# Chunk 0 of a three-stage kernel: a written order, filler products and wider queries

## The chip, the cores and the metric

The kernel runs on one core of a Trainium2 chip. Its engines work side by side, each through its own list of instructions in order: TensorE (PE: products, and its weight loads PEld), VectorE (DVE), ScalarE (ACT), GpSimd (POOL) and SyncE (SP, which here issues most DMAs). The metric is the device time of one execution in microseconds; lower is better.

## The reference

```python
kv  = einsum('bhsd,bhse->bhde', k, v)       # 8 batches, 8 heads, 576 tokens, 64 wide
out = einsum('bhsd,bhde->bhse', q, kv)
out = out / sqrt(mean(out*out, -1) + 1e-6) * g_norm
x   = out as [4608 tokens, 512]
h   = max(x @ w1, x @ w2, x @ w3)           # 512 -> 768
x   = h @ w_out                             # 768 -> 512
# then 8 experts: noisy gate, top 2 of 8, per expert relu(x @ w1[e]) @ w2[e], weighted sum
```

## The kernel before

The 4608 tokens are done in nine chunks of 512. For each chunk `ao` multiplies the queries with the K-V matrix of their batch, `norm_sq` (ACT, L230), `norm_red` (DVE, L234), `norm_b1` (DVE L238, then Ln and Exp on ACT L239 and L240), `norm_b2` (DVE, L244 to L246) and `norm_c` (DVE, L250) normalise it, `xtrans` turns it (PE L272) and splits it into a high and a low part (`xtrans_hi` ACT L276, `xtrans_lo` DVE L281). Projections are three products: high by high, and the two crossed ones. `g1` (L353) makes 18 groups of 128 columns, of which each three are joined by a maximum; `g2` (L399) is the output projection and the gate's logits. Chunks 1 to 8 run through `for g in range(18)` with the next chunk's attention woven in: at `g == 12` `attend` calls both halves of `ao`. After them the experts run, in units of up to 512 tokens.

`kv_all` makes the K-V matrix of a batch: 40 calls of `kv_mm` (L187), 32 of them with 128 tokens and 8 with the last 64. K and V of a batch come in three loads: `KV0`, `STG[2]` and `kvr`. A float32 call of `PE.matmul` becomes two load-and-product pairs in the trace. `ao(c, j)` (L213) does half a chunk, two blocks of 128 tokens; the held (stationary) operand is a piece of queries, 64 deep and 64 tokens wide, and the streamed one is the 64x64 K-V matrix of a head. A batch has 576 tokens, so 64 is the largest width that never meets two batches.

Chunk 0 has a schedule of its own, since the weights must be rebuilt first. Each of the twelve weight stages `s` arrives as 64-bit words (`w{s}`, SP) and goes through `lo` (ACT L502), `op` (DVE L506, L507), `sq` (ACT L511), `add` (DVE L515), `top` (DVE L528), `hi` (ACT L532) and `rest` (DVE L536). Meanwhile PE has the passes of chunk 0 (`first...`: groups 0 and 1 by halves of 256 tokens; `gp`, `gq`: groups 2 to 17), of the first half of chunk 1 (`eq`, with maxima `ee`), the second batch's K-V matrix (`kvp3`), chunk 1's `ao0` and `ao1`, the gate's weights (`gate_...`) and the output passes (`out...`). Each is a `task` with an engine, an assumed cost and the tasks it comes after; `run_tasks` lays them out greedily by those costs, and what it emits is each engine's order. Ahead of it stand the first loads, conversion of stage 0, K-V of batch 0, both halves of `ao` of chunk 0 and their first norm steps, and `warm(7)`, which are products (L576) whose result nobody reads.

Of the kernel before, what the change touches and what calls it, by code (L numbers as in the profile page):

```python
# [72 lines left out]
def unit_order():  # L73
    seq = [("S", 0), ("S", 1)]
    small = [("1", 0), ("2", 0), ("T", 1), ("1", 1)]
    for i in range(N4):
        seq.append(("4", i))
        if i % 2 and small:
            seq.append(small.pop(0))
    return seq + [("H", 0), ("J", 2), ("2", 1)], [("1", i) for i in range(N1_MAIN, N1)]  # L80


def body(tc, A, dbg=None):
# [81 lines left out]
    def qv(c):  # L165
        return qbuf[c][:, 0:2048].rearrange("p (a t) -> p a t", a=4)
# [4 lines left out]
    pad = st("pad", [128, XW])  # L171
    POOL.memset(ones, 1.0)
# [217 lines left out]
    def g2(c, i, f0, f1):  # L390
        if f0 == 0:
            x2b[i] = abank(), abank()
        s = slice(i * 128, (i + 1) * 128)
        for f in range(f0, f1):
            h = hTf(f)
            w = wo(f // 2)[:, :, f % 2]
            for n, (a, b) in enumerate(((0, 0), (0, 1), (1, 0))):
                for z, (lo, hi) in enumerate(((0, 256), (256, 528))):
                    PE.matmul(x2b[i][z][:, 0:hi - lo], h[:, a, s], w[:, b, lo:hi],  # L399
                              start=f == 0 and n == 0, stop=f == 5 and n == 2)  # L400
        if f1 == 6:
            DVE.tensor_copy(lgs[:, i, :], x2b[i][1][:, 256:272])
            for z in range(2):
                b = x2b[i][z].bitcast(U16).rearrange("p (n t) -> p n t", t=2)
                for q in range(2):
                    (ACT.copy if q else DVE.tensor_copy)(  # L406
                        planes[:, i, q * 512 + z * 256:q * 512 + z * 256 + 256], b[:, 0:256, q])

# [128 lines left out]

    def gate_a(j, ring):
        t, d = wsrc(9 + j), wstage(9 + j)
        for ff in range(2):  # L540
            TR = ring()
            for k in range(4):
                PE.transpose(TR[:, k * 128:(k + 1) * 128], t[:, ff * 512 + k * 128:ff * 512 + (k + 1) * 128], ident)
            ACT.activation(d[:, ff * 512:ff * 512 + 512], TR, AF.Copy)

    gate_of = {}
# [33 lines left out]
    load_q(0)  # L580
# [37 lines left out]
    tasks, ring_users = [], []  # L618

    def task(name, eng, cost, after, fn, urgency=0, hb=None):  # L620
        tasks.append((name, eng, cost, after, fn, urgency, hb))

    def run_tasks(free, end):
        while tasks:
            best = None
            for x in tasks:
                name, eng, cost, after, fn, urgency, hb = x
                need = list(after)
                if hb:
                    taken = ring_users + [hb] * hb[1]  # L630
                    need += [u[0] for u in taken[:-4]]
                if any(n not in end for n in need):
                    continue
                at = max([free[eng]] + [end[n][0] + 0.1 * (end[n][1] != eng) for n in need])
                key = (at, urgency)
                if best is None or at < best[0][0] - 0.3 or (at < best[0][0] + 0.3 and urgency < best[0][1]):
                    best = (key, x)
            assert best, [x[0] for x in tasks]
            (at, _), x = best
            tasks.remove(x)  # L640
            name, eng, cost, after, fn, urgency, hb = x
            fn()
            end[name] = at + cost + (2.0 if eng == "SP" else 0.0), eng
            free[eng] = at + cost
# [10 lines left out]
    task("n0b1", "DVE", 0.2, [], lambda: norm_b1(0, 0, 4), 0)  # L655
    task("n0e", "ACT", 0.5, ["n0b1"], lambda: None, 0)
    task("n0b2", "DVE", 0.65, ["n0e"], lambda: norm_b2(0, 0, 4), 0)
    for i in range(4):
        task(f"n0c{i}", "DVE", 0.65, ["n0b2"], lambda i=i: norm_c(0, i), 0)
# [4 lines left out]
        task(f"t0{i}", "PE", 0.44, [f"n0c{i | 1}"] + ([f"t0{i - 1}"] if i else []), t0, 0,  # L664
# [8 lines left out]
    task("kvp3", "PE", 2.3, ["kv1", "first100"], kv1, 1, on_ring("kvo", 4))  # L673
# [4 lines left out]
    for s in range(1, 12):  # L678
# [7 lines left out]
        task(f"lo{s}", "ACT", 1.15, [f"w{s}"] + ["n0e"] * (s == 1), lambda s=s: conv_lo(s), u)  # L686
        task(f"op{s}", "DVE", 1.92, [f"w{s}"] + free_t + ["n0c3"] * (s == 1), lambda s=s: conv_hi(s), u)
# [34 lines left out]
    for g in range(18):  # L722
        if g > 1:
            task(f"gp{g}", "PE", 1.82, ["x0l3", f"hi{g // 2}"] + done + ([f"gq{g - 1}"] if g > 2 else []),
# [3 lines left out]
        hm_free = [f"split{f - 1}"] if g % 3 == 0 and 0 < f < 4 else ["x1t1"] if g == 12 else []  # L728
# [10 lines left out]
    for i in range(2):  # L739
        if i == 0:  # L740
            task("ao0", "PE", 1.0, ["q1", "kvo", "x0l3", "ev0"] + done, lambda: ao(1, 0, [abank(), abank()]), 0)
        task(f"n1s{i}", "ACT", 0.6, ["ao0", "t03"], lambda i=i: norm_sq(1, i, x1[i]), 0.6)
        task(f"n1r{i}", "DVE", 0.69, [f"n1s{i}"], lambda i=i: norm_red(1, i), 0.6)
    task("n1b1", "DVE", 0.2, ["n1r0", "n1r1"], lambda: norm_b1(1, 0, 2), 0.5)
    task("n1e", "ACT", 0.5, ["n1b1"], lambda: None, 0.5)
# [16 lines left out]
    for e in range(18):  # L762
# [3 lines left out]
             [f"eq{e}", "x1t0", "x0h3"] + ([f"ee{e - 1}"] if e % 3 else []),  # L766
             lambda e=e: g1_top(e, bank_of["e", e][:, 0:256], early(e // 3)), 0.5)
    for j in range(3):
        task(f"gate_a{j}", "PE", 0.9, [f"top{9 + j}"] + ([f"gate_b{j - 1}"] if j else []),
             lambda j=j: gate_a(j, hbank), 1.5, on_ring(f"gate_a{j}", 2))  # L770
        task(f"gate_w{j}", "ACT", 1.2, [f"gate_a{j}"], lambda: None, 0)
# [10 lines left out]
    def ao_late():
        ao(1, 1, [hbank(), hbank()])
        for i in range(2):
            norm(1, 2 + i, RB[:, i * 512:i * 512 + 512])

    task("ao1", "PE", 1.0, ["rest11", "ao0"], ao_late, 3.5, on_ring("ao1", 2))
# [200 lines left out]
    for c in range(NCH):  # L988
# [425 lines left out]
def layout(q, k, v, g_norm, moe_w1, moe_w2, moe_w3, moe_w_out,  # L1414
# [6 lines left out]
    a["qT"] = qf.transpose(2, 1, 0, 3).reshape(NCH, 128, 2048)  # L1421
# [28 lines left out]
```

## Time and profile before

| | us |
|---|---|
| median of three timed runs | 1505.43 (1503.96 to 1508.12) |
| the profiled execution | 1503.61 |
| its span, first to last instruction | 1501.8 |
| PE busy in it | 1476.2 (98%) |
| DVE, ACT, POOL busy | 749.5, 644.2, 223.3 |
| mean granted clock of PE | 0.998 |

A busy PE is not PE at its peak: a product's end is modelled, and weight loads (PEld) lie beside products. Times in the rows are us from the span's start.

### The profile page before, as it was taken

What the parts mean: (1) busy time and instruction counts of PE and PEld (TensorE: products, weight loads), DVE (VectorE), ACT (ScalarE), POOL (GpSimd) and SP (SyncE); (2) the same over time, 40 slices, a digit from 0 to 9 for tenths busy, and PEclk for the clock granted to TensorE, in tenths of its full rate; (3) what the DMA queues carried; (4) which work ended last, traced back from release to release, by engine and by line L of the source; (5) the groups of instructions that cost most, each with busy time, mean ns of one, the idle gap of its engine ahead of it and who ended that gap; (6) DMA issues with size and microseconds to landing.
All of it is one profiled execution on the core that took longest, in us unless ns stands there. A gap on an engine that the chain in (4) does not pass through costs nothing.

```text
span 1501.8 us, 22899 instructions
## 1 busy us (share of the span) xinstructions
PE 1476.2 (98%) x9190; PEld 1260.4 (84%) x9190; DVE 749.5 (50%) x1513; ACT 644.2 (43%) x1020; POOL 223.3 (15%) x332
## 2 busy tenths in 40 slices
PE   6999999999999999999999999999999999999997
PEld 6889989898989888888888878887888888888886
DVE  6985545454444444458344454553454374444443
ACT  4653524242424233334444454544454364444443
POOL 0000111102020202023211102202211111110112
PEclk9999999999999999999999999999999999999999
DMA  7412435142332303083776668767565587554555
GB/s 315 144 70 99 152 117 149 72 149 86 126 114 99 121 29 122 0 240 107 200 200 140 173 217 227 194 186 199 135 162 137 147 216 196 132 135 140 139 121 108
DMA packets 160724, 218.43 MB, mean 145 GB/s; under 512 B 124320, under 2 KB 124704, under 8 KB 145120
## 3 DMA queue, kind: packets, MB, share of 16 engines
q1 hardware_dynamic: 140624, 165.14, 35.0%
q0 software_dynamic: 19984, 51.73, 15.1%
q8 instruction: 74, 1.21, 0.3%
q14 instruction: 42, 0.34, 0.1%
HBM read 137.86 MB, written 51.72 MB: 126 GB/s over the span
## 4 chain that ended last, share of the span: by engine, by line
PE 54%; POOL 0%; issue 0%; ACT 0%; POOLq 0%
PE bank L1242 26%; PE bank L1180 26%; PE bank L1194 1%; PE bank L1283 1%; PE bank L1298 0%; PE bank L399 0%; POOL out L1216 0%; PE bank L1205 0%; ACT W L334 0%; PE bank L1289 0%; ACT xn L1247 0%; POOLq L1398 0%; ACT RA L406 0%; PE bank L1136 0%; POOL spacer L1215 0%
## 5 line engine op out<-in xcount | busy, mean ns | idle before, releaser
L353 PE MATMUL bank<-B,W 128*128 128x512 f32 (+1 forms) x2184 | 453.1, 367 | 2.2 <-ACT W L532 2.1
L353 PEld LDWEIGHTS bank<-B,W 128*128 128x128 f32 x2184 | 376.4, 188 | 70.4 <-ACT W L532 2.5
L1242 PE MATMUL bank<-W,B 128*128 128x512 f32 x1704 | 411.2, 390 | 0.0
L1242 PEld LDWEIGHTS bank<-W,B 128*128 128x128 f32 x1704 | 318.6, 188 | 64.5
L1180 PE MATMUL bank<-B,W 128*128 128x512 f32 (+4 forms) x1536 | 361.0, 374 | 0.0
L1180 PEld LDWEIGHTS bank<-B,W 128*128 128x128 f32 x1536 | 278.1, 188 | 53.7 <-issue 4.4
L335 DVE TENSOR_TENSOR W<-G,W 128x1024 fp32r<-128x1024 f32 x168 | 203.0, 1224 | 121.8 <-ACT W L334 121.3
L1184 ACT ACTIVATE B<-bank 128x512 fp32r<-128x512 f32 (+4 forms) x152 | 85.8, 565 | 334.3 <-PE bank L1180 334.3
L1185 DVE SCALAR_TENSOR_TENSOR B<-bank,B 128x512 fp32r<-128x512 f32 (+4 forms) x152 | 98.7, 649 | 249.0 <-ACT B L1184 248.4
L334 ACT ACTIVATE W<-G 128x1024 fp32r<-128x1024 f32 x168 | 175.4, 1055 | 43.5 <-PE bank L1242 24.9
L399 PE MATMUL bank<-W,B 128*128 128x256 f32 (+1 forms) x1296 | 161.0, 284 | 0.4 <-DVE B L361 0.2
L399 PEld LDWEIGHTS bank<-W,B 128*128 128x128 f32 x1296 | 159.5, 188 | 1.6 <-ACT RA L406 0.5
L472 POOL DMA_INDIRECT Xg<-RA,si x72 | 70.7, 981 | 582.0 <-issue 403.7
L371 DVE TENSOR_TENSOR hm<-hm,bank 128x512 f32<-128x512 f32 (+1 forms) x107 | 69.6, 651 | 115.2 <-PE bank L353 109.8
L1216 POOL DMA_INDIRECT out<-xn,idt x36 | 59.2, 1644 | 402.9 <-ACT xn L1247 397.6
L357 ACT ACTIVATE B<-hm 128x512 fp32r<-128x512 f32 (+1 forms) x53 | 32.2, 607 | 172.4 <-DVE hm L371 172.4
L1180 PE MATMUL bank<-xlo,W 128*128 128x512 f32 (+2 forms) x288 | 73.3, 376 | 0.0
L1180 PEld LDWEIGHTS bank<-xlo,W 128*128 128x128 f32 x288 | 52.5, 188 | 9.8
L369 ACT ACTIVATE hm<-bank 128x512 f32<-128x512 f32 (+1 forms) x54 | 30.4, 564 | 64.1 <-PE bank L353 52.2
L406 ACT COPY RA<-bank 128x256 uint16<-128x256 uint16 x72 | 25.6, 372 | 68.6 <-DVE RA L406 63.2
L1216 POOL DMA_INDIRECT out<-hm,idt x20 | 31.9, 1593 | 131.2 <-ACT hm L1247 127.4
L361 DVE TENSOR_TENSOR B<-hm,B 128x512 fp32r<-128x512 f32 (+1 forms) x53 | 35.1, 661 | 32.2 <-ACT B L357 32.2
(230 smaller groups left out, 1034.8 us busy)
## 6 DMA issues: line engine op xcount, KB each, us to landing
G<-mw SPq DMA_DIRECT2D x84, 1024.0 KB, 5.1
G<-w1s SPq DMA_DIRECT2D x12, 1024.0 KB, 4.9
kv<-kv SPq DMA_DIRECT2D x8, 1024.0 KB, 7.1
G<-kv SPq DMA_DIRECT2D x8, 1024.0 KB, 9.2
RB<-qT SPq DMA_DIRECT2D x8, 1024.0 KB, 4.9
G<-mw SPq DMA_DIRECT2D x16, 512.0 KB, 6.4
out<-pad POOLq DMA_DIRECT2D x5, 1280.0 KB, 6.5
out<-pad POOLq DMA_DIRECT2D x2, 1536.0 KB, 6.7
```

Source lines behind the costliest of these rows:

```text
L334: ACT.activation(w[:, 0:1024], src, AF.Copy)
L335: DVE.tensor_tensor(w[:, 1024:2048], src, w[:, 0:1024].bitcast(F), op=OP.subtract)
L353: PE.matmul(bank[:, 0:t1 - t0], w_in(g)[:, a, k, s], x[b][:, k, t0:t1], start=n == 0 and k == 0, stop=n == 2 and k == 3)
L361: DVE.tensor_tensor(h[:, 1], hm, h[:, 0].bitcast(F), op=OP.subtract)
L371: DVE.tensor_tensor(hm, hm, bank, op=OP.max)
L399: PE.matmul(x2b[i][z][:, 0:hi - lo], h[:, a, s], w[:, b, lo:hi], start=f == 0 and n == 0, stop=f == 5 and n == 2)
L472: i = POOL.indirect_dma_start(out=Xg, out_offset=bass.IndirectOffsetOnAxis(ap=idx, axis=0), in_=src, in_offset=None)
L1180: PE.matmul(bank[:, 0:n], w[:, a, k, s], x[b][:, k, 0:n], start=z == 0, stop=z == 11)
L1184: ACT.activation(h[:, 0, 0:n], bank[:, 0:n], AF.Relu)
L1185: DVE.scalar_tensor_tensor(h[:, 1, 0:n], bank[:, 0:n], 0.0, h[:, 0, 0:n].bitcast(F), op0=OP.max, op1=OP.subtract)
L1216: d = POOL.indirect_dma_start(out=A["out"], out_offset=bass.IndirectOffsetOnAxis(ap=idt[u % 3][:, i:i + 1], axis=0), in_=y, in_offset=None ...
L1242: PE.matmul(obank[i], h[:, a, s], w[:, b, ff % 2, :], start=ff == 0 and n == 0, stop=ff == 7 and n == 2)
```

## The change

Chunk 0's attention also becomes tasks, cut so that each has one engine, and so are pieces of `gate_a`, `gate_d`, `g2` and of the norms of chunk 1. `run_tasks` no longer plans: it emits a written list, `ORDER`, and asserts that each task stands behind those it needs. Some needs are added to the graph. `empty` makes products of a zeroed tile ahead of K and V, between their halves and ahead of the queries; `warm` makes nine. The K-V products of batch 0 run by token block first. The queries are laid out in two halves, chunk 0's come in two loads, and `ao` holds 128 tokens at a time where both halves of a block are of one batch. The middle passes of `first...` change places.

```diff
+ORDER = """
+n0a0 n0s0 n0s1 n0a1 warm n0r0 n0r1 n0b10 n0s3 n0r3 n0s2 w1 n0r2 n0e0 n0b20 n0b11 n0e1 kv1 n0c1 n0c0 t00 x0h0 t01
+n0b21 w2 x0h1 n0c2 n0c3 t02 first000 x0l0 lo1 t03 first001 op1 x0h3 x0l3 first100 x0h2 first010 x0l2 x0l1 first110
+add1 sq1 lo2 top1 first011 kvp3 kvo q1 first002 op2 first101 first012 add2 w3 hi1 first111 first112 first102 ev0 gp2
+ev1 ao0 sq2 rest1 n1s1 n1s0 gq2 top2 hi2 n1r1 gp3 ev2 n1r0 gq3 n1b1 gp4 w4 n1e rest2 n1b2 n1c1 n1c0 hi_h0 x1t1
+split0 ev3 w5 op3 x1t0 gq4 x1h0 x1l0 x1h1 x1l1 ev4 lo3 sq3 gp5 gq5 lo4 eq0 add3 ev5 top3 eq1 eq2 ee0 op5 ee1 eq3 op4
+hi3 sq4 rest3 ee2 gp6 add4 ee3 eq4 hi_h1 top4 lo5 gq6 ee4 eq5 w6 gp7 gq7 split1 ee5 w7 ev6 add5 hi4 eq6 lo6 eq7 gp8
...
     def qv(c):
-        return qbuf[c][:, 0:2048].rearrange("p (a t) -> p a t", a=4)
+        return qbuf[c][:, 0:2048].rearrange("p (x a t) -> p x a t", x=2, a=4)
...
+    DVE.memset(XN[0], 0.0)
...
+    def empty(sizes):
+        for n in sizes:
+            PE.matmul(HB[3][:, 0:n], XN[0][:, 0:128], XN[0][:, 0:n], start=True, stop=True)
+
     def kv_all(b, banks):
-        for p in range(4):
-            for s in range(4):
-                kv_mm(b, p, s, banks[p][:, 0:64])
+        for p, s in ([(p, s) for s in range(4) for p in range(4)] if b == 0 else
+                     [(p, s) for p in range(4) for s in range(4)]):
+            if b == 0 and (p, s) == (0, 2):
+                empty([256] * 3)
+            kv_mm(b, p, s, banks[p][:, 0:64])
...
-                for x in range(2):
-                    t = t0 + x * 64
-                    kb = KB[(c * CT + t) // S % 2]
+                k = [KB[(c * CT + t) // S % 2] for t in (t0, t0 + 64)]
+                w = 128 if k[0] is k[1] else 64
+                for x in range(0, 128, w):
                     for h in range(2):
-                        PE.matmul(banks[h][HALF[x], o], qv(c)[HALF[h], p, t:t + 64],
-                                  kb[HALF[h], p * 64:(p + 1) * 64], start=True, stop=True)
+                        PE.matmul(banks[h][x:x + w, o], qv(c)[HALF[h], j, p, i * 128 + x:i * 128 + x + w],
+                                  k[x // 64][HALF[h], p * 64:(p + 1) * 64], start=True, stop=True)
...
-    load_q(0)
+    for i in range(2):
+        SP.dma_start(RB[:, i * 1024:i * 1024 + 1024], A["qT"][0][:, i * 1024:i * 1024 + 1024])
...
+    empty([512] * 4 + [320])
     first = [abank() for p in range(4)]
     kv_all(0, first)
+    empty([256])
     load_kv_first(1)
...
-    for j in range(2):
-        ao(0, j, [abank(), abank()])
-        for i in range(2):
-            norm_a(0, 2 * j + i)
-    warm(7)
...
+    def run_tasks(done):
+        for name in ORDER.split():
+            after, fn, hb = tasks.pop(name)
...
+            fn()
+            done.add(name)
...
+    for j in range(2):
+        task(f"n0a{j}", "PE", 1.05, [f"q0{j}"], lambda j=j: ao(0, j, [abank(), abank()]), 0)
+    task("warm", "PE", 4.05, ["n0a1"], lambda: warm(9), 0)
...
-    a["qT"] = qf.transpose(2, 1, 0, 3).reshape(NCH, 128, 2048)
+    a["qT"] = qf.reshape(4, 128, NCH, 2, 256).transpose(2, 1, 3, 0, 4).reshape(NCH, 128, 2048)
```

## Rows read from the trace of the kernel before

**Rows 1.** Waits of PE from 130 us on: line, releaser, total, times, longest.

```profile
PE bank L399 <- ACT RA L406: 0.2, 1, 0.2
```

**Rows 2.** Windows: stretch, busy us of each engine (instructions), granted clock, DMA.

```profile
10.50:14.60 4.10, 3.75 (x72) 3.50 (x72) 1.42 (x3) 1.14 (x2) 0.00 (x0) 1.00 0.95 374
27.70:30.00 2.30, 2.30 (x81) 2.20 (x80) 2.15 (x3) 1.25 (x1) 0.00 (x0) 1.00 0.00 0
```

**Rows 3.** Timeline of PE, 8 to 45 us: start, length, instructions, idle before and releaser.

```profile
8.26 0.69 PE L187 MATMUL bank<-kv 128*64 128x64 f32 x8 [8.26 <-DMA kv<-kv]
10.72 0.70 PE L187 MATMUL bank<-G 128*64 128x64 f32 x8 [1.77 <-DMA G<-kv]
...
13.91 0.56 PE L187 MATMUL bank<-hm 64*64 64x64 f32 x16
14.68 2.19 PE L213 MATMUL bank<-kvt,RB 64*64 64x64 f32 x128 [0.21 <-DVE kvt L198]
16.80 3.45 PE L576 MATMUL bank<-cst 128*128 128x270 f32 x14
21.61 1.48 PE L272 MATMUL bank<-cst,xn 128*128 128x128 f32 x10 [1.35 <-DVE xn L250]
...
23.83 3.97 PE L353 MATMUL bank<-B,W 128*128 128x256 f32 x28
...
36.56 3.02 PE L353 MATMUL bank<-B,W 128*128 128x512 f32 x12
41.67 2.11 PE L353 MATMUL bank<-B,W 128*128 128x512 f32 x8 [2.09 <-ACT W L532]
```

**Rows 4.** Timeline of PE in chunk 1: both halves of `ao` for chunk 2.

```profile
154.00 2.10 PE L213 MATMUL bank<-kvt,RB 64*64 64x64 f32 x128
```

**Rows 5.** Weight loads of the span by form: operand, count, busy us, mean ns.

```profile
L353 PEld LDWEIGHTS bank<-B,W 128*128 128x128 f32 x2184 | 376.4, 188 | 70.4 <-ACT W L532 2.5 <-issue 1.2 <-DVE B L281 0.3
...
L213 PEld LDWEIGHTS bank<-kvt,RB 64*64 64x64 f32 x1024 | 15.8, 135 | 2.6 <-issue 2.1 <-DVE kvt L198 0.3
...
L1136 PEld LDWEIGHTS bank<-cst,s 128*1 128x1 f32 x2 | 0.2, 82 | 0.2
```

**Rows 6.** Timeline of weight loads near 101 us: the four of one `gate_d`.

```profile
101.35 0.54 PEld L561 LDWEIGHTS bank<-cst,G 128*128 128x128 f32 x4
```

**Rows 7.** Timeline of SP's queue at the head: issue, its length.

```profile
2.15 0.77 SPq L571 DMA_DIRECT2D hm<-kvr  x1
2.96 0.48 SPq L169 DMA_DIRECT2D RB<-qT  x1
```

**Rows 8.** The same two DMAs: size and us from issue to landing.

```profile
RB<-qT SPq DMA_DIRECT2D x1, 1024.0 KB, 10.9
hm<-kvr SPq DMA_DIRECT2D x1, 256.0 KB, 9.2
```

**Rows 9.** Timeline of ACT, 15 to 42 us.

```profile
15.98 1.57 ACT L230 ACTIVATE xn<-bank 128x512 f32<-128x512 f32 x3 [1.13 <-PE bank L213]
...
22.48 2.46 ACT L276 ACTIVATE B<-bank,gn 128x512 fp32r<-128x512 f32 x4 [1.63 <-PE bank L272]
...
40.56 1.06 ACT L532 ACTIVATE W<-RA 128x1024 fp32r<-128x1024 f32 x1
```

**Rows 10.** Timeline of DVE, 20 to 41 us.

```profile
20.30 0.19 DVE L246 SCALAR_TENSOR_TENSOR stat<-stat 128x32 f32<-128x32 f32 x1
20.59 1.89 DVE L250 TENSOR_TENSOR xn<-bank,stat 128x512 f32<-128x512 f32 x3
...
35.57 0.69 DVE L371 TENSOR_TENSOR hm<-hm,bank 128x512 f32<-128x512 f32 x1
37.31 0.69 DVE L234 TENSOR_REDUCE stat<-xn 128x8 f32<-128x512 f32 x1 [1.05 <-ACT xn L230]
...
39.31 1.22 DVE L528 SCALAR_TENSOR_TENSOR RA<-G 128x1024 f32<-128x1024 f32 x1
```

More of the change, by code (lines that the diff above doesn't have):

```diff
@@ L234, in norm_red, with norm_b1, norm_e @@
         DVE.tensor_reduce(ST[:, 0, i, :], x.rearrange("p (h e) -> p h e", h=8), axis=AX.X, op=OP.add)
-    def norm_b1(c, i0, i1):
+    def norm_b1(c, i0, i1, now=True):
         s = [ST[:, r, i0:i1, :] for r in range(2)]
         DVE.tensor_scalar(s[0], s[0], 1.0 / 64, 1e-6, op0=OP.mult, op1=OP.add)
+        if now:
+            norm_e(c, i0, i1)
+    def norm_e(c, i0, i1):
+        s = [ST[:, r, i0:i1, :] for r in range(2)]
         ACT.activation(s[1], s[0], AF.Ln)
@@ L400, in g2, with g2_out @@
                               start=f == 0 and n == 0, stop=f == 5 and n == 2)
-        if f1 == 6:
-            DVE.tensor_copy(lgs[:, i, :], x2b[i][1][:, 256:272])
[L403 to L407, printed above, removed]
+        if f1 == 6 and (c > 0 or i > 1):
+            for q in range(2):
+                g2_out(i, q)
+    def g2_out(i, q):
+        if q == 0:
+            DVE.tensor_copy(lgs[:, i, :], x2b[i][1][:, 256:272])
+        for z in range(2):
+            b = x2b[i][z].bitcast(U16).rearrange("p (n t) -> p n t", t=2)
+            (ACT.copy if q else DVE.tensor_copy)(
+                planes[:, i, q * 512 + z * 256:q * 512 + z * 256 + 256], b[:, 0:256, q])
     lgs = st("lgs", [128, 4, 16])
@@ L536, in conv_rest, with gate_w @@
         DVE.tensor_tensor(lo, t, hi.bitcast(F), op=OP.subtract)
+    gate_of = {}
     def gate_a(j, ring):
-        t, d = wsrc(9 + j), wstage(9 + j)
-        for ff in range(2):
-            TR = ring()
+        t = wsrc(9 + j)
+        gate_of["a", j] = [ring() for ff in range(2)]
+        for ff, TR in enumerate(gate_of["a", j]):
             for k in range(4):
                 PE.transpose(TR[:, k * 128:(k + 1) * 128], t[:, ff * 512 + k * 128:ff * 512 + (k + 1) * 128], ident)
-            ACT.activation(d[:, ff * 512:ff * 512 + 512], TR, AF.Copy)
-    gate_of = {}
+    def gate_w(j):
+        for ff, TR in enumerate(gate_of["a", j]):
+            ACT.activation(wstage(9 + j)[:, ff * 512:ff * 512 + 512], TR, AF.Copy)
     def gate_b(j, ring):
@@ L610, in zero_out @@
                            pad.bitcast(U16).unsqueeze(1).to_broadcast([128, 4, 2 * XW]))
-    for j in range(2):
-        ao(0, j, [abank(), abank()])
-        for i in range(2):
-            norm_a(0, 2 * j + i)
-    warm(7)
-    tasks, ring_users = [], []
-    def task(name, eng, cost, after, fn, urgency=0, hb=None):
[L621 to L644, printed above, removed]
+    tasks, ring_users = {}, []
+    def task(name, eng, cost, after, fn, urgency=0, hb=None):
+        tasks[name] = after, fn, hb
+    def run_tasks(done):
+        for name in ORDER.split():
+            after, fn, hb = tasks.pop(name)
+            taken = ring_users + [hb] * (hb[1] if hb else 0)
+            for n in after + [u[0] for u in taken[:-4] if hb]:
+                assert n in done, (name, n)
             if hb:
                 ring_users.extend([hb] * hb[1])
+            fn()
+            done.add(name)
+        assert not tasks
     bank_of, tr0 = {}, {}
@@ L654, in body @@
     task("kv1", "SP", 6.0, ["w1"], lambda: None, 1)
-    task("n0b1", "DVE", 0.2, [], lambda: norm_b1(0, 0, 4), 0)
-    task("n0e", "ACT", 0.5, ["n0b1"], lambda: None, 0)
-    task("n0b2", "DVE", 0.65, ["n0e"], lambda: norm_b2(0, 0, 4), 0)
+    for j in range(2):
+        task(f"n0a{j}", "PE", 1.05, [f"q0{j}"], lambda j=j: ao(0, j, [abank(), abank()]), 0)
+    task("warm", "PE", 4.05, ["n0a1"], lambda: warm(9), 0)
     for i in range(4):
-        task(f"n0c{i}", "DVE", 0.65, ["n0b2"], lambda i=i: norm_c(0, i), 0)
+        j = i // 2
+        task(f"n0s{i}", "ACT", 0.5, [f"n0a{j}"], lambda i=i: norm_sq(0, i, XNS[i]), 0)
+        task(f"n0r{i}", "DVE", 0.65, [f"n0s{i}"], lambda i=i: norm_red(0, i), 0)
+    for j in range(2):
+        task(f"n0b1{j}", "DVE", 0.2, [f"n0r{2 * j}", f"n0r{2 * j + 1}"], lambda j=j: norm_b1(0, 2 * j, 2 * j + 2, False), -1)
+        task(f"n0e{j}", "ACT", 0.5, [f"n0b1{j}"], lambda j=j: norm_e(0, 2 * j, 2 * j + 2), -1)
+        task(f"n0b2{j}", "DVE", 0.62, [f"n0e{j}"], lambda j=j: norm_b2(0, 2 * j, 2 * j + 2), 0)
+    for i in range(4):
+        task(f"n0c{i}", "DVE", 0.65, [f"n0b2{i // 2}"], lambda i=i: norm_c(0, i), 0)
         def t0(i=i):
             tr0[i] = xtrans_pe(0, i)
-        task(f"t0{i}", "PE", 0.44, [f"n0c{i | 1}"] + ([f"t0{i - 1}"] if i else []), t0, 0,
+        task(f"t0{i}", "PE", 0.44, [f"n0c{i & 2}", f"n0c{i | 1}"] + (["warm"] if i == 0 else [f"t0{i - 1}"]), t0, 0,
              on_ring(f"x0l{i}"))
@@ L685, in body @@
         u = 2 + 0.1 * s if s > 1 else 0.4
-        task(f"lo{s}", "ACT", 1.15, [f"w{s}"] + ["n0e"] * (s == 1), lambda s=s: conv_lo(s), u)
-        task(f"op{s}", "DVE", 1.92, [f"w{s}"] + free_t + ["n0c3"] * (s == 1), lambda s=s: conv_hi(s), u)
+        task(f"lo{s}", "ACT", 1.15, [f"w{s}"] + ["n0e1"] * (s == 1), lambda s=s: conv_lo(s), u)
+        task(f"op{s}", "DVE", 1.92, [f"w{s}"] + free_t + ["n0a0", "n0a1"] * (s < 3), lambda s=s: conv_hi(s), u)
         task(f"sq{s}", "ACT", 1.14, [f"op{s}"], lambda s=s: conv_sq(s), u - 1 if s > 1 else 0.05)
@@ L740, in body @@
         if i == 0:
[L741 to L745, printed above, removed]
+            task("ao0", "PE", 1.0, ["q1", "kvo", "x0l3", "ev0", "ev1"] + done, lambda: ao(1, 0, [abank(), abank()]), 0)
+        task(f"n1s{i}", "ACT", 0.6, ["ao0", "t02", "t03"], lambda i=i: norm_sq(1, i, x1[i]), 0.6)
+        task(f"n1r{i}", "DVE", 0.69, [f"n1s{i}"] + [f"n0c{k}" for k in range(4)], lambda i=i: norm_red(1, i), 0.6)
+    task("n1b1", "DVE", 0.2, ["n1r0", "n1r1"], lambda: norm_b1(1, 0, 2, False), 0.5)
+    task("n1e", "ACT", 0.5, ["n1b1"], lambda: norm_e(1, 0, 2), 0.5)
     task("n1b2", "DVE", 0.65, ["n1e"], lambda: norm_b2(1, 0, 2), 0.5)
@@ L774, in body @@
         task(f"gate_d{j}", "PE", 0.5, [f"gate_c{j}", f"rest{9 + j}"], lambda j=j: gate_d(j, hbank), 1.5,
-             on_ring(f"gate_d{j}"))
+             on_ring(f"gate_f{j}"))
+        task(f"gate_e{j}", "ACT", 0.2, [f"gate_d{j}"], lambda j=j: gate_ef(j, False), 0)
+        task(f"gate_f{j}", "DVE", 0.19, [f"gate_e{j}"], lambda j=j: gate_ef(j, True), 0)
         for i in range(2):
             task(f"out{i}{j}", "PE", 1.5,
-                 [f"gate_d{j}", f"split{2 * j + 1}", "gq17"] + (["rest11", "gate_a2"] if j == 2 else [])
-                 + ([f"out{i}{j - 1}"] if j else []),
+                 [f"gate_f{j}", f"split{2 * j}", f"split{2 * j + 1}", "gq17"] + (["rest11", "gate_a2"] if j == 2 else [])
+                 + ([f"out{i}{j - 1}"] if j else []) + ["out0" + str(j)] * i,
                  lambda i=i, j=j: g2(0, i, 2 * j, 2 * j + 2), 4 + 0.1 * j + 0.01 * i)
[L782 to L787, printed above, removed]
+    x1.update({i: RB[:, (i - 2) * 512:(i - 1) * 512] for i in (2, 3)})
+    task("ao1", "PE", 1.0, ["rest11", "ao0"], lambda: ao(1, 1, [hbank(), hbank()]), 3.5, on_ring("n2c3", 2))
+    for i in (2, 3):
+        task(f"n2s{i}", "ACT", 0.6, ["ao1", "add10", "add11"], lambda i=i: norm_sq(1, i, x1[i]), 0.6)
+        task(f"n2r{i}", "DVE", 0.69, [f"n2s{i}"], lambda i=i: norm_red(1, i), 0.6)
+    task("n2b1", "DVE", 0.2, ["n2r2", "n2r3"], lambda: norm_b1(1, 2, 4, False), 0.5)
+    task("n2e", "ACT", 0.5, ["n2b1"], lambda: norm_e(1, 2, 4), 0.5)
+    task("n2b2", "DVE", 0.65, ["n2e"], lambda: norm_b2(1, 2, 4), 0.5)
+    for i in (2, 3):
+        task(f"n2c{i}", "DVE", 0.65, ["n2b2"] + ["n2c2"] * (i > 2), lambda i=i: norm_c(1, i), 0.5)
+    for i in range(2):
+        task(f"pd{i}", "DVE", 0.95, [f"out{i}2"], lambda i=i: g2_out(i, 0), 0.4)
+        task(f"pa{i}", "ACT", 0.75, [f"out{i}2"], lambda i=i: g2_out(i, 1), 0.4)
+    task("fin", "PE", 0.0, ["out12", "pd0", "pa0", "n2c3"], lambda: None, 9)
     order, spare = unit_order()
@@ L999, in body @@
         if c == 0:
-            run_tasks({"PE": 16.8, "DVE": 19.0, "ACT": 18.2, "SP": 13.5, "POOL": 10.0},
-                      {f"{n}0": (12.0, "DVE") for n in ("w", "lo", "op", "sq", "add", "top", "hi", "rest")})
+            run_tasks({f"{n}0" for n in ("w", "lo", "op", "sq", "add", "top", "hi", "rest")} | {"q00", "q01"})
         window(c)
```

41 lines of the change are left out of this document (27 added, 14 removed).

## The prediction

> **What bounds the kernel now.** I read the page's slices first: TensorE (PE) is full nearly throughout. Then the list of PE's waits: from 130 us to the end it holds one wait, of 0.2 us [rows 1]. So from there on every microsecond that PE's instructions take more or less shows in the span. What PE loses stands at the head, and PE's timeline [rows 3] tells where: 8.26 us until the first K and V have landed, 1.77 us for their second half, 1.35 us for normed rows (with 14 filler products of `warm` ahead of it, which do no work), 2.09 us at 41.67 for a converted weight (L532). From 41.67 on PE has no gap that matters.
>
> The windows show a second loss at the head. The 72 products of `kv_mm` between 10.50 and 14.60 were 3.75 us long, 52 ns each; the same products in 27.70 to 30.00 were 2.30 us for 81, 28 ns each [rows 2]. [...]
>
> So two sums: what the head gives back, and what the changed products cost where PE is never idle.
>
> **`ao`, 128 tokens held at a time: the largest term.** A half of a chunk (`ao(c, j)`) is now 32 calls. A float32 call is two load-and-product pairs, so a chunk has 128, and they took 2.10 us at 154 us [rows 4]; a half is 1.05 us. The operands are 64x64, on a quarter of the array: (token half, depth half) gives four places, and each place gets 16 of the half's 64 pairs. After the change the held operand is 64x128, so there are two places (depth half), and 32 pairs: again 16 for each place. Halving the instructions therefore saves nothing by itself; what counts is how long one place needs for a pair. Today that is at most 1.05 us / 16 = 66 ns, and about 57 ns without some 0.14 us of start and end.
>
> A pair is a stream of 64 columns, unchanged, and a load, which doubles. The loads by shape [rows 5]: 82 ns for 1 column, 135 for 64, 188 for 128. That is 82 ns of fixed latency and 0.83 ns a column, so the load itself is 53 ns for 64 columns and 107 for 128. Is it hidden when the stream is short? The nearest row: four loads of 128 columns for products of only 16 columns (L561) take 0.54 us, the last of them 0.19, so they follow each other every (0.54 - 0.19) / 3 = 117 ns [rows 6]. There the load sets the pace. With 117 ns a step against 57, a half costs 16 x 0.060 = 0.96 us more, a block of 128 tokens 0.48; I take 115 ns, 0.46 us a block.
>
> The blocks: chunks 1 to 8 have 32. Four of them (one in each of chunks 1, 3, 5, 7) hold a batch boundary, which falls at an odd multiple of 64 tokens, and keep width 64. So 28 x 0.46 = **13.0 us** are added, all inside stretches where PE doesn't wait.
>
> Bounds, as no row shows a 64x128 load. From below nothing: if loads hid behind the stream, 16 steps of 57 ns stay; a gain is excluded, since a place still streams 16 times the same columns. From above: products of 256 columns (L353), where load and stream are about equal, took 0.14 us each (28 from 23.83 to 27.73, [rows 3]); 141 ns a step makes 28 x 8 x 0.084 = 18.8 us. Should the two depth halves load one after the other, a step is 230 ns and the term 39 us; the 64x64 row speaks against that, since 128 loads of 53 ns in 2.10 us need over three places loading at once.
>
> [...]
>
> **The head: K, V and queries.** `empty` multiplies zeroed `XN[0]` until K and V land. DVE's memset ahead of it costs nothing: DVE then has nothing to do until the first weights are in. Its sizes add up to 2368 columns; `warm` needs 0.49 us for 270 (3.45 / 7, [rows 3]), so 4.3 us at that pace and 8.6 at half. If it starts near 1 us, as the loads do, it ends at 5.3 to 9.6. K's first half lands at 8.26, but PE then waits anyway until 10.72, so even the late end costs nothing. After 10.72 only 48 products remain (32 and 16) instead of 72, at 28 ns if the fill has kept the pace: about 1.4 us, ending at 12.1 where `kv_mm` ended at 14.47. The first half of the queries lands: `kvr` issued at 2.15 took 9.2 us (11.35), the queries issued at 2.96 took 10.9 (13.86) [rows 7, 8], so half of that megabyte is in at 12.6, the rest at 13.9. `n0a0` can start at 12.7, 2.0 us before 14.68.
>
> Then the chain, with halves of 1.95 us: 12.7 to 14.65 to 16.6 (before: 16.80). Squares take 0.52 us each on ACT and began 0.15 us after the half they read (three in 1.57, [rows 9]). ACT's list puts Ln and Exp of the first pair behind all four squares, so: squares to 15.9, the other two 16.75 to 17.85, Ln and Exp (some 0.5 together) to 18.35; on DVE three small operations (0.2 each) and two of `norm_c` (0.63 each) to 20.75 [rows 10]. The nine products of `warm` (0.49 each) end at 21.05 and set `t00`, against 21.61 before. From `t00` to the first projection product it was 2.22 us; two transposes, two copies of 0.61 [rows 9] and their latencies make 2.1. So 23.2 instead of 23.83: **0.6 us earlier**.
>
> From there to `gp4` PE's work is the same (48 products of 256 columns, `kv_mm`, four passes, `ao0`), but `t03` now stands behind the first product (0.3 us), and ACT's list has `lo1` (1.1 us) ahead of the copies that `first010` needs (a wait of 0.45).
>
> The wait of **2.09 us** for `hi2` goes if `top2` comes sooner. Before, it started at 39.31 on DVE. The list now puts `ev2`, `n1r0`, `n1r1`, `n1b1` and `split0` behind it, and the 1.05 us wait for a square with them; that is all that DVE did from 35.57 to 39.31 (five instructions, the first two shown in [rows 10]), and the work ahead of 35.57 is the same as before. So `top2` can start at 35.57 and `hi2` ends at 35.57 + 1.23 + 1.06 = 37.9, not at 41.62 [rows 9, 10]. PE wants it at 39.58, where its products before the wait end [rows 3], give or take the microsecond that this part moves it: covered by over 1 us. What comes late next is the conversion after that, and there PE has 13 us of other products (`gp4`, `gq4`, `gp5`, `gq5`, four `eq`) before `gp6`.
>
> Head: 0.6 + 2.09 - 0.45 - 0.3 = **1.9 us gained**. Ends: 0 if the pace of `kv_mm` stays at 52 ns (below), 3.2 if `ao` keeps its pace, because the halves then end 1.7 us sooner and the chain 1.25.
>
> **The rest at nothing.** `norm_b1`, Ln, Exp and `norm_b2` twice for chunk 0: five DVE instructions of under 0.2 us and two on ACT, counted in the chain. `gate_a`, `gate_d` and `g2_out` cut into pieces: the same instructions, on ACT and DVE, while PE has products in hand. The `tri` load now stands behind `w9` on SP; `fills` on POOL waits for it, and nothing reads that before chunk 1's routing near 144 us. One DMA more on SP's queue is 0.5 us of issue ahead of the constants, whose turn on the full DMA engines comes later anyway.
>
> **Sum.** -1.9 + 13.0 = +11.1 us. The profiled execution took 1503.6 us (span 1501.8 and 1.8 around it), the median is 1505.4, 1.8 above it. So 1514.7 by the profile, and **1516.5** as the median.
>
> **Rivals.**
> *A, the forecast:* loads of 128 columns set the pace of `ao`; 1516.5. Chance 0.60, with 1512 to 1522 as its own range (107 to 141 ns a step, head 0 to 3).
> *B, the other side:* the wide load hides (another place loads while this one streams, and the load of the next pair starts early). Then only the head counts, -3.2 us: 1502.2; with up to 2 us more if the chain of pair 0 runs ahead, 1500. In between, each ns a step is worth (13.0 + 1.25) / 58 = 0.25 us, so the sign turns at 57 + 3.2 / 0.25 = 70 ns a step. For it: 53 ns of stream and 53 of load already overlap today. Against it: L561. Chance 0.29.
> *C:* the two depth halves load in turn: 39 us in the blocks, and the head's gain is gone; about 1545. Chance 0.05.
> *D, the fill does nothing:* zeros do not raise the pace, so `kv_mm` stays at 52 ns and the fill itself is slow. Its second part (768 columns, 2.8 us at half pace, from 9.9 on) then ends near 12.7, the 48 products at 15.2, and the chain loses about 2.8 us against A: 1519. Chance 0.06, and the slow side of A's range holds it.
>
> Under 0.3% (4.5 us) a measurement of this kernel can't be told from no change. A is slower but for 0.04 (a step near 75 ns); B is divided, 0.13 faster by more than 4.5 us, because the order of the list may remove small waits I did not cost, and 0.16 within; C and D are slower. So faster 0.13, same 0.20, slower 0.67. The range 1500 to 1523 leaves out C and the far end of B.
>
> **What would show it.** A: `ao` of one chunk takes near 3.8 us instead of 2.10, its loads are 188 ns long, and two of them start every 115 ns; `first000` starts near 23.2; no wait for L532 at `gp4`. B: `ao` stays near 2.1 us. D: the 48 products after 10.7 are 52 ns each. I am wrong if `ao` is not slower, or if PE has waits of microseconds between 45 and 130 us, where I count none.

## The result, and the profile after

The changed kernel takes 1513.04 us (median, 1512.15 to 1518.39) against 1505.43: a ratio of 1.0057, 95% interval 1.0041 to 1.0073. It is slower by 0.57%, outside what can't be told from no change. The profiled execution took 1514.09 us with a span of 1512.3, 10.5 more than before; 1516.5 had been forecast as the median.

First the list of PE's waits (line, releaser, total us, times, longest), whole run of the changed kernel:

```profile
PE bank L210 <- DVE xn L190: 1.5, 1, 1.5
PE bank L1283 <- DVE B L1226: 1.1, 2, 0.6
PE bank L206 <- DMA kv<-kv: 0.6, 1, 0.6
PE bank L383 <- ACT B L306: 0.4, 1, 0.4
PE bank L302 <- DVE xn L280: 0.2, 1, 0.2
```

The waits of the head are gone: 1.77, 1.35 and 2.09 us in [rows 3]. PE's list of waits is some 10 us shorter, but 8 of these are no gain: the products of zeros (the fills, L210) now stand where PE waited 8.26 us for the first K and V, which are used at 8.09 all the same. PE waits less and the kernel is slower, so the loss lies in work. The profiled execution of before lay 1.8 us under its median and this one 1.1 above, which is why the spans differ by more (10.5) than the medians (7.6). The 1.1 us near the end (L1283) is in this execution and not in that of before; whether other executions have it isn't shown.

PE's timeline of the head (start, length, instructions, idle before):

```profile
8.09 1.15 PE L206 MATMUL bank<-kv 128*64 128x64 f32 x32 [0.58 <-DMA kv<-kv]
...
10.66 1.15 PE L206 MATMUL bank<-G 128*64 128x64 f32 x32
11.74 0.46 PE L206 MATMUL bank<-hm 64*64 64x64 f32 x16
...
12.83 3.79 PE L238 MATMUL bank<-kvt,RB 64*128 64x64 f32 x64
16.54 4.36 PE L615 MATMUL bank<-cst 128*128 128x270 f32 x18
20.74 1.04 PE L302 MATMUL bank<-cst,xn 128*128 128x128 f32 x8
...
22.70 0.74 PE L383 MATMUL bank<-B,W 128*128 128x256 f32 x4
```

K-V is done at 12.2 instead of 14.47, the queries' products start at 12.83 instead of 14.68 and end at 16.54 instead of 16.80: almost all that was gained ahead of them is spent in them. The first projection product starts at 22.70, before at 23.83.

The same products in chunk 1, for chunk 2 (the line that answers to [rows 4]), and what follows them:

```profile
151.93 3.79 PE L238 MATMUL bank<-kvt,RB 64*128 64x64 f32 x64
155.65 8.90 PE L383 MATMUL bank<-B,W 128*128 128x256 f32 x72
```

Half as many pairs, and 3.72 us from start to start against 156.03 - 154.00 = 2.03. The loads of the same products, before and after (PEld's timeline):

```profile
154.00 1.96 PEld L213 LDWEIGHTS bank<-kvt,RB 64*64 64x64 f32 x128
151.93 3.65 PEld L238 LDWEIGHTS bank<-kvt,RB 64*128 64x128 f32 x64
```

By the forecast's places, four before and two after, the chunk has 32 rounds both times. No row shows a place by itself; with the forecast's 53 and 107 ns a load (its estimate from [rows 5]) the loads are 128 x 53 = 6.8 us in 1.96, so 3.5 at a time, and 64 x 107 = 6.8 us in 3.65, so 1.9 (estimates). Without the last load (135 and 188 ns) a round takes (1.96 - 0.135) / 31 = 59 ns before and (3.65 - 0.188) / 31 = 112 ns after. The loads by form (count, busy us, mean ns), to set beside [rows 5]:

```profile
L238 PEld LDWEIGHTS bank<-kvt,RB 64*128 64x128 f32 x464 | 26.7, 188 | 2.8 <-issue 2.1 <-DVE kvt L223 0.4
...
L238 PEld LDWEIGHTS bank<-kvt,RB 64*64 64x64 f32 x96 | 1.7, 134 | 0.2
```

For 128 columns it is 188 ns on 64 rows and 189 on 128 rows (L383); for 64 columns 134 on 64 rows and 138 on 128 (L206). So the rows make little difference to these loads; it isn't the columns alone, since the loads of 128 rows and 128 columns at L578 took 140.

The account, by where the same instruction stands in the two traces. Chunk 1 begins at 131.86 instead of 133.93: 2.1 us gained, although chunk 1's own wide products already took 1.4 us of it. The experts' first product stands at 684.59 instead of 676.02: 8.6 us lost. Between them lie 25 wide blocks at (3.72 - 2.03) / 4 = 0.42 us, 10.6 us, and 10.6 - 2.1 = 8.5. Behind that point another 1.9 us go, 1.1 of them in the waits at L1283 shown above; the rest isn't traced.

### The profile page after: what moved, and what is told of

It is laid out like the page before. It is cut to its first block, busy times and chain, and to the rows that moved or that the text cites. A ratio compares the mean times of both kernels' runs of the same rounds, so it can differ in the third digit from the quotient of the medians.

```text
span 1512.3 us, 21930 instructions
## 1 busy us (share of the span) xinstructions
PE 1497.3 (99%) x8700; PEld 1276.5 (84%) x8700; DVE 750.1 (50%) x1514; ACT 644.1 (43%) x1020; POOL 222.8 (15%) x332
## 3 DMA queue, kind: packets, MB, share of 16 engines
q8 instruction: 70, 1.15, 0.3%
## 4 chain that ended last, share of the span: by engine, by line
PE 96%; DMA 1%; DVE 1%; ACT 0%; issue 0%; POOL 0%; POOLq 0%; SPq 0%; DVEq 0%
PE bank L383 29%; PE bank L1283 26%; PE bank L1221 25%; PE bank L429 10%; PE bank L238 2%; PE bank L206 1%; PE bank L1235 1%; DMA G<-mw 1%; PE bank L1324 0%; PE bank L1339 0%; DMA kv<-kv 0%; DMA G<-w1s 0%; PE bank L302 0%; PE bank L578 0%; POOL out L1257 0%
## 5 line engine op out<-in xcount | busy, mean ns | idle before, releaser
L383 PE MATMUL bank<-B,W 128*128 128x512 f32 (+1 forms) x2184 | 452.5, 367 | 0.4 <-ACT B L306 0.4
L383 PEld LDWEIGHTS bank<-B,W 128*128 128x128 f32 x2184 | 376.1, 189 | 67.7 <-issue 0.8
L1283 PE MATMUL bank<-W,B 128*128 128x512 f32 x1704 | 412.0, 390 | 1.1 <-DVE B L1226 1.1
L1283 PEld LDWEIGHTS bank<-W,B 128*128 128x128 f32 x1704 | 318.3, 188 | 66.7 <-DVE B L1226 2.0
L399 ACT ACTIVATE hm<-bank 128x512 f32<-128x512 f32 (+1 forms) x54 | 30.5, 566 | 74.6 <-PE bank L383 61.2
```

What stands on the lines that cost most here:

```text
L1283: PE.matmul(obank[i], h[:, a, s], w[:, b, ff % 2, :], start=ff == 0 and n == 0, stop=ff == 7 and n == 2)
```

## The experiments

The runs come in three groups, made on different chips (the kernel before: 1505.7 in the first, 1511.1 in a single run of the second, 1510.6 in the third), so medians are compared within a group. The ratios are to the kernel before, over all executions of the group, and so differ a little from the quotient of two medians. One landmark serves for all traces: the first product of chunk 1's routing, 144.00 us before and 141.92 after.

**First group: which part costs, which part gives.**

The change with 64 tokens held again:

```diff
-                w = 128 if k[0] is k[1] else 64
+                w = 64
```

> The changed kernel with the queries held 64 tokens at a time again, all else kept. Theory L (the load of 128 held columns sets the pace of the attention products): a chunk's products fall from 3.72 us back to about 2.05; 28 blocks of chunks 1 to 8 give back 0.42 us each, 11.8 us, and the chain of chunk 0 about 1 more, so about 1501 us (1499.5 to 1503), faster than the kernel before. Rival R (the order of chunk 0, the fills or the cut pieces make the change slow): it stays near 1513, or gives back only part of the 7.6 us.

Measured: 1506.54 us, ratio 1.0007 (0.9997 to 1.0018). So the wide products are what made the kernel slower, and a chunk's products are back at 2.1 us, as theory L has it. But 6.5 us come back and not some 12: of the 4 us that the rest should have gained nothing is left, so rival R (the order or the fills) holds in part, and the runs without the fills show why. The landmark stands at 146.23, 2.2 us later than before the change.

The kernel before with 128 tokens held, nothing else (the same loop of `ao`, on the old layout):

> The kernel before with the queries held 128 tokens at a time, nothing else changed. Theory L: 3.72 us for a chunk's products, 28 blocks of 0.42 us and 1 to 3 us in the chain of chunk 0, less what the 2.09 us wait of chunk 0 hides: 1516 to 1520. Rival R: 1505, no change.

Measured: 1521.86 us, ratio 1.0110 (1.0093 to 1.0127), the landmark at 148.04. This is theory L alone and above its range: 28 blocks of 0.42 make 11.8 us, and the head lost 4.0 us to the landmark, chunk 1's three blocks among them. Its trace also has two waits that the one of before has not, 1.0 us at L399 and 0.7 at L1242. Rival R is out.

The change with 64 tokens and without the products of zeros:

```diff
     def empty(sizes):
-        for n in sizes:
+        for n in ():
```

> The changed kernel, 64 tokens at a time, with the products of zeros taken out. If the fills keep the pace of the K-V products (28 ns each): without them they take 52 ns again, the queries' products start about 1.3 us later and all behind them 1 to 2 us later than in the kernel with the fills. If the fills are worth nothing: within 0.3 us of it at the start of chunk 1.

Measured: 1500.29 us, ratio 0.9971 (0.9960 to 0.9983), the landmark at 141.20. Both expectations fail: the kernel without the fills is 6 us *faster* than with them, and 5 us of it are there at the landmark. And the kernel before with the fills, the K-V order and the two loads of queries, but its own order:

```diff
+    empty([512] * 4 + [320])
     first = [abank() for p in range(4)]
     kv_all(0, first)
+    empty([256])
```

> The kernel before with only the fills, the K-V order by token block and the queries in two loads; the planned order stays, 64 tokens at a time. If the head's gain comes from there: chunk 0's products of queries start 2 us sooner, and chunk 1 starts 1.3 to 2.2 us sooner, the wait for a converted weight (2.09 us) staying: about 1503.5. If the gain is the written order's: chunk 1 starts within 0.5 us of before.

Measured: 1507.11 us, ratio 1.0012 (1.0003 to 1.0021), the landmark at 146.79: 2.8 us later instead of 1.3 to 2.2 sooner. These edits bring the queries' products forward by 1.9 us (12.82 against 14.68) and lose more behind them. PE's timeline of the change with 64 tokens shows where:

```profile
11.85 0.46 PE L206 MATMUL bank<-hm 64*64 64x64 f32 x16
12.24 0.70 PE L210 MATMUL bank<-xn 128*128 128x256 f32 x2
12.94 2.20 PE L238 MATMUL bank<-kvt,RB 64*64 64x64 f32 x125
19.29 0.48 PE L238 MATMUL bank<-kvt,RB 64*64 64x64 f32 x3 [4.15 <-issue]
19.70 6.88 PE L615 MATMUL bank<-cst 128*128 128x270 f32 x18
```

Three products from the end of its list of 128, PE stops for 4.15 us, and no engine or DMA of the kernel released it ("issue"). The windows of the same trace (busy us, then granted clock and DMA) show the rest:

```profile
14.00:16.00 2.00, 1.14 (x69) 1.00 (x61) 1.22 (x2) 1.08 (x2) 0.00 (x0) 1.00 0.87 336
16.00:18.00 2.00, 0.00 (x0) 0.00 (x0) 0.23 (x2) 0.00 (x0) 0.00 (x0) 1.00 1.05 434
18.00:20.00 2.00, 0.71 (x4) 0.59 (x5) 0.00 (x0) 0.19 (x1) 0.00 (x0) 0.50 0.97 410
20.00:22.00 2.00, 2.00 (x5) 1.55 (x5) 1.53 (x4) 1.21 (x4) 0.00 (x0) 0.50 1.00 421
22.00:24.00 2.00, 2.00 (x6) 1.44 (x5) 1.88 (x8) 0.43 (x2) 0.00 (x0) 0.50 1.08 415
24.00:26.00 2.00, 2.00 (x9) 1.58 (x8) 1.40 (x3) 0.00 (x0) 0.00 (x0) 0.79 0.60 254
26.00:28.00 2.00, 1.89 (x15) 1.52 (x13) 0.23 (x1) 0.95 (x2) 0.00 (x0) 1.00 0.05 12
```

After the idle stretch the granted clock is 0.50 until 24 to 26 us: the warm products take 6.71 us from start to start instead of 4.20, and the turning of the rows waits behind them. That is the second price of this stop. It isn't paid at each one: of the stops told of below, the clock also fell behind the one of 2.68 us (0.50 from 20 to 22; the 14 warm pairs there are 5.14 us long against 3.45 in [rows 3]), but stayed at 1.00 behind those of 1.10 and 2.46.

What stops PE? Count the pairs up to it: 18 of zeros, 80 of K-V, 125 of queries, 223. In the kernel before with fills the stop (2.68 us) comes after 18 + 80 + 125, again 223. In the one without fills:

```profile
13.27 2.19 PE L238 MATMUL bank<-kvt,RB 64*64 64x64 f32 x128 [0.21 <-DVE kvt L223]
15.39 3.68 PE L615 MATMUL bank<-cst 128*128 128x270 f32 x15
20.18 0.95 PE L615 MATMUL bank<-cst 128*128 128x270 f32 x3 [1.10 <-issue]
```

80 + 128 + 15 is 223 too, at another line and another time. A fourth program below (64 tokens held, a longer stream) stops after 18 + 80 + 125 as well. So the place is a number of instructions, 446 loads and products.

And the time? The profile has a DMA queue of its own for instructions, with packets of 16 KB: 74 of them in the kernel before, for its 9190 pairs, and 70 after the change, for 8700, so one for 124 pairs in both. Their number follows PE's list, so I take them for PE's program. The first of them in the span lies ahead of each restart by nearly the same time:

| kernel | its first 16 KB packet begins | PE goes on | between |
|---|---|---|---|
| before with fills | 15.42 | 17.79 | 2.37 |
| 64 tokens, longer stream | 16.63 | 18.88 | 2.25 |
| 64 tokens, fills | 17.00 | 19.29 | 2.29 |
| 64 tokens, no fills | 17.95 | 20.18 | 2.23 |

So the account that fits all four is that PE had run to the end of the program that it held, and went on 2.2 to 2.4 us after the next part began to come. That is my reading: no trace shows what PE holds. What sets the packet's start isn't shown: data transfers keep the DMA engines at 0.87 to 1.08 in that stretch, but no run changes them.

In the kernel before, PE had issued 222 pairs (80, 128 and 14) by 20.25 us. Its packet begins at 18.19, so by the lag of the table (an estimate) the next part was there at 20.5, within the wait for DVE that ends at 21.61: by this reading the limit cost nothing there, and no row of PE shows it. The changed kernel has issued 18 + 80 + 64 + 18 = 180 by 20.74; its packet begins at 17.89, long before its 224th pair.

So the fills don't make the next part come later; they move the stop to where more work stands behind it. Without them PE goes on at 20.18, later than the 19.29 with them, but has only three of the 18 pairs of `warm` left to do. With them three pairs of queries and all 18 of `warm` are left, at the lower clock.

**Second group: is it the load?** One execution each, read by the products' own rows. Three of four products stream 128 columns instead of 64 (the extra columns are overwritten by the next product):

```diff
+                n = 64 if p == 3 else 128
...
-                        PE.matmul(banks[h][x:x + w, o], ...
-                                  k[x // 64][HALF[h], p * 64:(p + 1) * 64], start=True, stop=True)
+                        PE.matmul(banks[h][x:x + w, o.start:o.start + n], ...
+                                  k[x // 64][HALF[h], p * 64:p * 64 + n], start=True, stop=True)
```

> The changed kernel with 128 columns streamed instead of 64 in three of four products of the attention (the next head pair's columns too, overwritten by the next product; the last keeps 64): the loads stay, the stream is 1.75 times as long. Theory L: the stream lies under the load of 128 columns; a chunk's products stay at 3.7 to 4.3 us. Rival S (the stream or the write of 128 rows sets the pace): 6.3 to 6.5 us.

```profile
155.24 3.79 PE L239 MATMUL bank<-kvt,RB 64*128 64x128 f32 x64
158.96 3.26 PE L384 MATMUL bank<-B,W 128*128 128x256 f32 x25
```

3.72 us from start to start with 1.75 times the stream, exactly as without: the stream lies wholly under the loads. Rival S (6.3 to 6.5) is out. The same with 64 tokens held:

> The same longer stream with 64 tokens held. Theory L: a load of 64 columns is 53 ns and a stream of 128 is 107, so the stream now sets the pace: 3.4 to 3.7 us for a chunk instead of 2.05. Rival S: 3.4 to 3.6 as well; this run is the other half of the comparison with the 128-token form.

```profile
13.12 3.30 PE L239 MATMUL bank<-kvt,RB 64*64 64x128 f32 x125
18.88 0.33 PE L239 MATMUL bank<-kvt,RB 64*64 64x64 f32 x3 [2.46 <-issue]
```

3.30 for 125 pairs where 64 streamed columns took 2.20, or 3.30 / 125 x 4 = 106 ns a pair for each of four places: with the short load the stream sets the pace. The 107 ns that theory L gave for a stream of 128 columns, like the forecast's 53 for 64, came without a row; the changed kernel's 18 warm pairs of 270 columns take 4.20 us, 0.86 ns a column, so some 111 and 55 (an estimate). Both theories had said so; the run is the other half of the comparison. And here too the stop comes after 18 + 80 + 125 pairs. Last, each product cut in two of 32 columns, which doubles the loads at the same stream:

> The changed kernel with each attention product of 64 streamed columns cut into two of 32, so that the loads of 128 columns double while the streamed columns stay. Theory L: a chunk's products double, 7.3 to 7.6 us instead of 3.72. Rival S: 3.7 to 4.2 us.

Its time as a whole was 1585.53 us. In chunk 0 the 128 pairs took 9.36 us and near 643 us 11.15, more than the 7.3 to 7.6 of theory L, but not at one clock. The windows of that run:

```profile
15.00:17.00 2.00, 2.00 (x40) 2.00 (x38) 0.00 (x0) 0.11 (x1) 0.00 (x0) 1.00 0.98 406
...
19.00:21.00 2.00, 2.00 (x23) 2.00 (x22) 0.01 (x1) 0.00 (x0) 0.00 (x0) 0.50 1.03 430
```

At clock 1.00 it is 2.00 / 38 = 53 ns a load, or 105 for a place, as theory L has it; then the clock falls to 0.50 in the middle of these products, with no idle time, and a load takes 2.00 / 22 = 91 ns. So the run supports the load, and its size was missed because of the clock, which theory L had not in it.

**Third group: the head without its new limit.** Wide products in chunk 0 alone:

```diff
-                w = 128 if k[0] is k[1] else 64
+                w = 128 if c == 0 else 64
```

> The changed kernel with 128 tokens held in chunk 0 alone, 64 in chunks 1 to 8, the fills kept. Theory P (two effects: each block of 128 held tokens costs 0.42 us where PE never waits; in chunk 0 the wide form keeps PE short of its 224th product until the next part of its program has come): no wait for issue at the head, and 28 x 0.42 = 11.8 us less than the changed kernel, 1500 to 1502. If the wait of 4.15 us has nothing to do with the number of products, but comes with the 64x64 products behind the fills, it is absent here too; the next run tells these apart.

Measured: 1504.96 us, ratio to the kernel before 0.9967 (0.9953 to 0.9980); on the first group's scale, 1505.7 x 0.9967, that is 1500.7, as expected. The landmark is at 140.69, and there is no wait for issue at the head. PE's list has such waits elsewhere:

```profile
PE bank L206 <- issue: 1.5, 4, 0.4
PE bank L238 <- issue: 1.0, 1, 1.0
```

The four stand among the K-V products of another batch (147.0 to 149.6 us), the fifth in queries' products at 574 us. Every trace of the second and third groups has four like these, and none of the first group has them, nor have those before and after the change. So PE stops for "issue" not only at the head. Whether the chip makes the difference between the groups isn't shown, as the kernel before has no trace in the later ones. With 32 tiny products of zeros in the changed kernel:

```diff
     empty([256])
+    for n in range(32):
+        PE.matmul(HB[3][0:1, 0:2], XN[0][:, 0:1], XN[0][:, 0:2], start=True, stop=True)
     load_kv_first(1)
```

> The changed kernel with 32 tiny products of zeros (2 columns, 64 pairs in the trace) ahead of the queries' products of chunk 0, all else kept. Theory P: PE comes to its 224th product within the queries' products, as in the run with 64 tokens, and waits for issue until 19 to 20 us; then the granted clock falls and chunk 1 starts 3 to 6 us later than in the changed kernel: 1516 to 1519. Rival: only the 1 to 2 us of the tiny products themselves, no wait for issue.

Measured: 1525.57 us, ratio 1.0089 (1.0067 to 1.0110), the landmark at 148.59, 6.7 us later. On the first group's scale that is 1519.1, nearly the time of theory P, but its reason is not:

```profile
12.84 1.74 PE L631 MATMUL bank<-xn 128*1 128x2 f32 x64
14.51 6.25 PE L238 MATMUL bank<-kvt,RB 64*128 64x64 f32 x64
20.69 6.83 PE L615 MATMUL bank<-cst 128*128 128x270 f32 x18
```

There is no wait for issue at the head. The granted clock falls to 0.50 around 15.5 us instead, behind the tiny products (the changed kernel's stays at 1.00 there), and the wide ones take 6.25 us instead of 3.79. The 224th pair comes near 20 us, and the 16 KB packet began at 15.47, so by the lag of the table (an estimate) the next part of the program is there near 17.8. So this run doesn't test the stop; what it shows is that these 64 tiny pairs as a fill cost the clock. The wide form in chunk 0 without the fills (both edits above):

> As the first run (128 tokens held in chunk 0 alone), without the fills. Where PE doesn't run out of its program, the fills should be worth what the pace of the K-V products gives: queries' products about 0.5 us later, chunk 1 0.5 to 1 us later than with them. If the fills harm by themselves (clock, power), this run is 3 us or more faster than the first.

Measured: 1508.84 us, ratio 0.9984 (0.9971 to 0.9997), the landmark at 140.67, the same as with fills.

```profile
8.14 1.98 PE L206 MATMUL bank<-kv 128*64 128x64 f32 x32 [8.14 <-DMA kv<-kv]
10.59 1.62 PE L206 MATMUL bank<-G 128*64 128x64 f32 x32 [0.47 <-DMA G<-kv]
12.90 3.79 PE L238 MATMUL bank<-kvt,RB 64*128 64x64 f32 x64 [0.31 <-DVE kvt L223]
```

In the trace the queries' products start at 12.90 instead of 12.95, not 0.5 us later as expected. The K-V products are slower (1.98 and 1.62 us for 32, against 1.15) and lose nothing here, because PE then waits for DVE's copies of the K-V matrix (L223); these stand behind a conversion (L569) that ends near 12.7 in both kernels. With 64 tokens held and no fills the K-V products take 1.98 us twice, and the queries start at 13.27 against 12.94 with fills.

The timed median is 3.9 us behind that with the fills (2.6 by the ratios), over a wide spread: four of twelve executions lie at 1503.7 to 1504.6, the traced one among them, and six at 1510.2 to 1511.8. No trace shows why; that is left open. So in this form the fills do no harm, and whether they help isn't settled. With 64 tokens but for the second half of chunk 0 (`w = 128 if c == 0 and j == 1 else 64`):

> 64 tokens held everywhere but in the second half of chunk 0's queries. Theory P: 32 pairs more than the first run, so PE comes to its 224th product only behind the warm products, near 21 us, when the next part of its program has just come; the first half ends 0.85 us sooner. 0 to 1 us faster than the first run, if the wait for issue stays under 0.5 us.

Measured: 1505.72 us, ratio 0.9968 (0.9957 to 0.9980), the landmark at 140.76. 64x64 products right behind the fills, 32 pairs more than in the first run of this group, and no stop: so the form isn't what stops PE in the run with 64 tokens throughout. The gain of up to 1 us that was expected isn't there: the first projection product starts 0.7 us sooner, and PE then waits 0.7 us for the next chunk's queries (`L238 <- DMA kv<-qT`), which gives it back.

## Why the prediction was right, step by step

- **`ao`, 13.0 us.** Right, and by its reason: the load of 128 columns sets the pace (3.72 us for a chunk against 3.8 forecast, loads of 188 ns). The size was a little high, 0.42 us a block instead of 0.46, so 11.8. The loads of a place follow each other every 112 ns rather than 115, and before every 59 rather than 57.
- **K-V and the start of the queries.** Right: 12.83 against 12.7, the halves to 16.54 against 16.6. But the credit to the fills was wrong, and so this term came out right by luck. Without them the queries start at 12.90 (128 tokens in chunk 0) and 13.27 (64 tokens), so of the 1.85 us from 14.68 the fills bring some 0.3 at most. What is left is the order of K-V by token block and the two loads of queries, which no run takes apart; the pace of the last 48 products is nearly hidden under DVE's copies.
- **The chain to `first000`.** 22.70 against 23.2; 0.2 of it is that nine warm products take 4.20 us and not 4.41. The wait of 0.45 for `lo1` behind it was there, with 0.41 (`L383 <- ACT B L306`).
- **The wait of 2.09 us.** Gone as argued; `hi2` ends at 37.98, forecast 37.9.
- **The head, 1.9 us.** Chunk 1 starts 2.1 us sooner with 1.4 us of wide products in it, so 3.5. The term was low by 1.6. Half a microsecond of it is the chain to `first000`. As much was in two waits of 0.24 us each that the kernel before had at 108 and 121 us (L543, L399), which were counted as nothing and are gone. Another 0.4 is that 32 projection products took 4.90 us (29.27 to 34.17) where they had taken 5.33 (30.14 to 35.47); no run shows why, and the last 0.2 isn't traced.
- **Sum.** +11.1 in the forecast, +10.5 in the profiled spans, +7.6 in the medians. The terms as measured, 11.8 - 3.5, make +8.3. The range of 1500 to 1523 would have held rival B's 1502.2 too; that the reason was right is seen in the products' rows, not in the range.
- **Rival B** was priced at 1502.2. The kernel whose `ao` keeps its old pace, with all else of the change, takes 1506.5. The step that failed is the one that took PE's list as ready whenever its operands are: PE stopped after 223 pairs. No row shown of the trace before holds this limit, since by the estimate above PE reached it in the same stretch as a wait for DVE. In the forecast case it was not met, only because the wide form needs 64 pairs less in chunk 0; that is luck.
- **Rival D** (zeros don't raise the pace) is out: K-V's first 32 pairs are 1.15 us long behind the fills and 1.98 without. Their loads are 138 ns behind the fills and 225 without (the median in the kernel before, from 10.7 to 13.6, is 227), while the clock column reads 1.00 in both, so it doesn't show this difference.

## What to carry to other kernels

Fewer instructions are not less work where a small product's weight load sets the pace, as here: 64 pairs that load 128 columns took 3.72 us, 128 pairs that load 64 took 2.03. So count loaded columns for each place, not products. A filler's pairs count too: in four programs here PE stopped for "issue" after 223 pairs, those of the filler among them where it had one. At a kernel's start, count how many instructions PE has got through when it stops so, and see what stands behind that place. (That either carries over to other kernels isn't shown here.) Here, keeping the narrow form outside chunk 0 turns a loss of 0.57% into a gain of 0.33%; keeping it everywhere and leaving out the fills gains 0.29%, the same within the intervals.

## What the runs showed of the hardware that had not been expected

- PE stopped after exactly 223 load-and-product pairs in four programs, for 1.1 to 4.15 us, and went on 2.2 to 2.4 us after a 16 KB packet on the instruction queue had begun.
- The granted clock fell to 0.50 not only after idle time (18 to 24 us in the run with the stop of 4.15) but also without any: amid 128 products of 32 columns, and behind 64 tiny ones.
- A 64-row load of 128 columns is 188 ns in the trace, a 128-row one at L383 189, and streaming 128 columns instead of 64 under it changed 3.72 us by nothing.
